# One slot for both halves of an output projection's weights, and the first half's matmuls moved behind the last attention unit

## The chip, the cores and the metric

The kernel runs on one core of a Trainium2 chip. The metric is the device time of one execution in microseconds (us), the median of several. Most runs were timed in five rounds, turn about with the kernel before on the same chip.

In the views, PE is TensorE (matmuls), PEld its weight loads, DVE VectorE, ACT ScalarE, and SPq the queue of SyncE, which issues the loads. PSUM is the memory into which TensorE accumulates. A slot is a buffer of a tile pool, and a load into it waits until the last reader of what was there is done. The granted clock is the share of TensorE's full clock that the profile records: 1.00 or 0.50 here.

## The reference, cut to what matters

One token for each of two batch rows passes a layer with two parallel branches. The attention branch projects the normalized x to 32 heads (wq), attends over the last 2048 rows of a K and a V cache with 16 heads, and projects back with wo (4096 x 576). The MLP branch has w1 (576 x 4608), a squared ReLU, and w2 (4608 x 576).

```
xn = layernorm(x)
q = xn @ wq;  p = softmax(q @ k.T / sqrt(128));  o = p @ v      # 2 x 16 heads of K and V, 2048 rows
h = relu(xn @ w1 + b1) ** 2
out = x + o @ wo + h @ w2 + b2
```

Each weight and each cache row is read once: 53.62 MB, almost all of it bf16, for two rows of output.

## The kernel before

Attention goes in 8 units of 2 MB of K and 2 MB of V. `step(u)` transposes K of unit u, and in between does the softmax of unit u-1 and PV (softmax weights times V) of an earlier unit. `pv_out(u)` takes a unit's result to its place (the rows `sm<-acc` in the timelines), and after every fourth unit `ws` is ready for one half of wo. Both halves of wo, the first three groups of w2 (nine 128-row blocks each) and the residual are accumulated in `out_ps`. The fourth group of w2 goes to another PSUM tile in four quarters that work side by side, so that little is left to do after the last load; the rest is then added to it (`part`).

```python
kvpool = ctx.enter_context(tc.tile_pool(name="kvpool", bufs=6))      # K, V and w2 groups
wbig = ctx.enter_context(tc.tile_pool(name="wbig", bufs=1))          # wq, then w1, then w2's last group
wopool = ctx.enter_context(tc.tile_pool(name="wopool", bufs=1))      # one half of wo
# ...
def out_acc(lhsT, rhs_of, start=False, stop=False):
    for i in range(2):
        pe_mm(out_ps[32 * i:32 * i + B, :], lhsT=lhsT, rhs=rhs_of(i * OH, (i + 1) * OH), ...)
# ...
def wo_acc(tq):                      # WR = 16 rows, 32 matmuls
    ws = wo_state.pop(tq)
    wo_sb = wo_tiles.pop(tq)
    for r in range(WR):
        out_acc(ws[:, r, :], lambda a, z: wo_sb[:, r, a:z])
# ...
issue_wo(1)                          # all loads of a kind go out on one queue
for w in W2P:
    issue_w2(*w)
wo_acc(0)
step(NU - 1, NU - 3, NU - 4)         # the last unit's K
# ... PV and softmax of the last two units ...
pv_all(NU - 1)
pv_out(NU - 1)
mlp_o(*W2P[0])
wo_acc(1)
for w in W2P[1:NG4 - 1]:
    mlp_o(*w)
# ... part <- out_ps; mlp_tail(rows 0 to 6); add part; mlp_tail(rows 7, 8); casts; store
```

## Time and profile before

| | kernel before |
|---|---|
| median of the first three runs | 134.18 us (134.14 to 134.27) |
| span in the profile | 132.5 us |
| TensorE busy | 91.7 us, 69% |
| transfers, share of 16 engines' time | 94.8% (the load queue) |
| end of the accumulation in `out_ps`, by the start of its copy | 127.61 us |
| release of the last w2 group's first piece | 128.43 us |

The prediction below shows the views that carry the argument. One more is wanted here: what the load queue itself waited for. Its columns are the waiting engine and line, the releaser, and the total, the number and the longest of the waits.

```profile
SPq L118 <- DMA wo<-in_A_wo_dram: 10.2, 1, 10.2
SPq L131 <- PE kT_ps L87: 8.8, 1, 8.8
SPq L118 <- PE out_ps L84: 3.4, 1, 3.4
```

Line 118 issues wo, line 131 w2 (which waits for slots of K tiles in use). The second half of wo waits for the first half to land (10.2 us) and then for its matmuls (3.4 us), because there is one slot. Such a wait of the issuing queue costs nothing as long as enough transfers are already under way.

### The profile page before, as it was taken

How to read it: one execution, taken by the hardware profiler on the slowest of the kernel's cores; microseconds unless marked ns; L12 is line 12 of the kernel's file. 1: busy time of each engine (PE TensorE's matmuls, PEld its weight loads, DVE VectorE, ACT ScalarE, POOL GpSimd, SP SyncE). 2: the span in 40 equal slices, each digit the busy share in tenths (PEclk: the TensorE clock that was granted, in tenths of full speed). 3: DMA queues.
4: the chain of work that ended last, by engine and by line, in shares of the span. 5: the costliest groups of instructions: out<-in, count | busy, mean ns of one | idle time of the engine just before them, and what ended most of it. 6: DMA issues, size and time to landing. Idle time of an engine off the chain costs nothing.

```text
span 132.5 us, 2040 instructions
## 1 busy us (share of the span) xinstructions
PE 91.7 (69%) x830; PEld 56.6 (43%) x830; DVE 59.7 (45%) x151; ACT 43.9 (33%) x63; POOL 7.7 (6%) x26
## 2 busy tenths in 40 slices
PE   0069228789762949879789389799285996449971
PEld 0059102639421439645366075465053653114540
DVE  6944301224640006565765823788700338744021
ACT  2707401016700044748357137367000733200001
POOL 7700000001000001010010000010100000100000
PEclk9999986856999595999999958999965579975698
DMA  3999989999998999999999999999999999999950
GB/s 105 443 445 501 389 381 430 430 483 513 401 403 359 430 410 455 411 460 401 465 396 445 425 415 453 415 456 432 423 410 445 415 440 433 414 432 423 418 216 1
DMA packets 3632, 53.74 MB, mean 406 GB/s; under 512 B 412, under 2 KB 420, under 8 KB 680
## 3 DMA queue, kind: packets, MB, share of 16 engines
q1 hardware_dynamic: 3604, 53.61, 94.8%
q8 instruction: 6, 0.10, 0.3%
q10 hardware_dynamic: 20, 0.01, 0.0%
q14 instruction: 2, 0.02, 0.0%
HBM read 53.62 MB, written 0.00 MB: 405 GB/s over the span
## 4 chain that ended last, share of the span: by engine, by line
DMA 71%; PE 21%; DVE 2%; ACT 2%; issue 1%; SPq 1%; DVEq 0%; ACTq 0%
DMA k<-in_A_k_cache_dram 44%; DMA w<-in_B_w_dram 13%; DMA wq_sb<-in_A_wq_dram 13%; PE kT_ps L87 10%; PE sc_ps L84 4%; PE q_ps L84 3%; PE qs_ps L84 1%; PE pv_ps L84 1%; DVE kT L288 1%; PE tail_ps L84 1%; PE sm L84 1%; ACT kT L286 1%; ACT pr L325 1%; DVE qrow L252 1%; SPq L106 0%
## 5 line engine op out<-in xcount | busy, mean ns | idle before, releaser
L87 PE MATMUL kT_ps<-ident_f,k 128*128 128x128 f32 x256 | 41.7, 322 | 6.3 <-DMA k<-in_A_k_cache_dram 6.2
L286 ACT COPY kT<-kT_ps 128x1024 bf16<-128x1024 bf16 x32 | 32.0, 1011 | 36.4 <-PE kT_ps L87 34.2
L87 PEld LDWEIGHTS kT_ps<-ident_f,k 128*128 128x128 f32 x256 | 35.2, 168 | 15.2 <-issue 12.0
L288 DVE COPY kT<-kT_ps 128x1024 bf16<-128x1024 bf16 x32 | 22.1, 692 | 31.9 <-PE kT_ps L87 31.7
L84 PE MATMUL sc_ps<-kT,qz 128*32 128x512 bf16 x128 | 10.5, 413 | 4.2 <-DVE kT L288 2.8
L84 PE MATMUL pv_ps<-v,pT 128*32 128x512 bf16 x128 | 10.9, 405 | 1.0 <-DVE acc L360 0.8
L314 POOL PARTITION_ALL_REDUCE gmax<-m x8 | 2.9, 366 | 104.3 <-DVE m L312 104.3
L84 PE MATMUL out_ps<-wo,ws 128*2 128x288 bf16 x64 | 6.8, 391 | 2.8 <-DMA wo<-in_A_wo_dram 2.8
L84 PEld LDWEIGHTS <-xnT 128*4 128x4 bf16 x90 | 3.1, 116 | 12.9 <-issue 12.7
L325 ACT ACTIVATE pr<-sc_ps,nb 128x512 bf16<-128x512 f32 x8 | 5.5, 687 | 8.1 <-DVE nb L322 8.1
L84 PE MATMUL q_ps<-wq_sb,xnT 128*4 128x512 bf16 x36 | 3.6, 573 | 4.9 <-DMA wq_sb<-in_A_wq_dram 4.9
L310 DVE TENSOR_REDUCE mx<-sc_ps 128x1 f32<-128x512 f32 x8 | 5.5, 684 | 3.1 <-PE sc_ps L84 3.1
L84 PE MATMUL h_ps<-w_sb,xnT 128*4 128x384 bf16 x54 | 4.3, 483 | 3.7 <-DMA w_sb<-in_B_w_dram 3.7
L84 PEld LDWEIGHTS <-qz 128*32 128x32 bf16 x128 | 2.3, 98 | 9.7 <-DVE kT L288 6.4
L84 PE MATMUL sm<-acc,tohead 128*64 128x129 f32 x16 | 4.0, 334 | 3.5 <-DVE acc L360 3.5
L84 PEld LDWEIGHTS <-ws 128*2 128x2 bf16 x64 | 3.7, 112 | 5.8 <-issue 3.1
L360 DVE SCALAR_TENSOR_TENSOR mix<-pv_ps,own_j,mix 128x128 f32<-128x128 f32 x16 | 5.6, 351 | 0.6
L87 PE MATMUL pro_ps<-ident,xs 2*128 2x2 bf16 x10 | 0.6, 164 | 7.6 <-DVE xs L182 7.6
L331 DVE STREAM_TRANSPOSE pT<-pr 128x512 bf16<-128x512 bf16 x8 | 5.6, 701 | 0.0
L566 ACT CAST fin_sb<-tail_ps 2x144 bf16<-2x144 f32 x2 | 0.5, 272 | 14.8 <-PE tail_ps L84 14.7
L433 DVE TENSOR_TENSOR hs<-hT_ps,hodd 128x20 f32<-128x20 f32 (+1 forms) x4 | 0.5, 173 | 10.3 <-ACT hodd L430 10.3
L84 PEld LDWEIGHTS <-pT 128*32 128x32 bf16 x128 | 2.7, 95 | 5.6 <-issue 3.0
(77 smaller groups left out, 60.4 us busy)
## 6 DMA issues: line engine op xcount, KB each, us to landing
k<-in_A_k_cache_dram SPq DMA_DIRECT2D x8, 2048.0 KB, 7.7
v<-in_A_v_cache_dram SPq DMA_DIRECT2D x8, 2048.0 KB, 17.1
w_sb<-in_B_w_dram SPq DMA_DIRECT2D x1, 5184.0 KB, 19.5
wq_sb<-in_A_wq_dram SPq DMA_DIRECT2D x1, 4608.0 KB
wo<-in_A_wo_dram SPq DMA_DIRECT2D x2, 2304.0 KB
w<-in_B_w_dram SPq DMA_DIRECT2D x3, 1296.0 KB, 19.4
w<-in_B_w_dram SPq DMA_DIRECT2D x1, 1008.0 KB
w<-in_B_w_dram SPq DMA_DIRECT2D x1, 288.0 KB
```

What stands on the lines that cost most here:

```text
L84: return tc.keep_in_program_order(nc.tensor.matmul(out, **kw))
L87: return tc.keep_in_program_order(nc.tensor.transpose(**kw))
L252: nc.vector.tensor_copy(out=qrow[:, 0, :], in_=q_ps[0][0:RB, :])
L286: pin(nc.scalar.copy(out=dst, in_=src))
L288: pin(nc.vector.tensor_copy(out=dst, in_=src))
L310: pin(nc.vector.tensor_reduce(out=mx[:], in_=sc_ps, axis=AX.X, op=ALU.max))
L314: nc.gpsimd.partition_all_reduce(gmax[:], m2[:], channels=P, reduce_op=ReduceOp.max)
L325: pin(nc.scalar.activation(out=pr[:], in_=sc_ps, func=ACT.Exp, bias=nb[:], scale=scale, accum_out=acc[:, Dh:Dh + 1]))
L331: pin(nc.vector.transpose(out=pT[:].rearrange("p t m -> p (t m)"), in_=pr[:]))
L360: op = nc.vector.scalar_tensor_tensor(out=nx, in0=pv_ps[:, j, :], scalar=own_j[:, j:j + 1], in1=acc, op0=ALU.mult, op1=ALU.add)
L433: nc.vector.tensor_tensor(out=hs[:].rearrange("p (g r) b -> p r g b", g=NG4)[:, r0:r0 + n, g:g + 2, :], in0=even[:, :, g:g + 2, :], in1=od ...
L566: cp(out=fin_sb[:, q * OQ:(q + 1) * OQ], in_=mlp["out"][32 * k:32 * k + B, :])
```

## The change

The intent: `wo_acc(0)` stands ahead of the last unit's transposes, though TensorE has idle time later, in the waits of the last PV. To move it there, the second half of wo must no longer wait for the first half's slot. Both halves together fit the slot that w1 leaves, and w2's last group, which had that slot, goes to a K/V slot. The pieces of the last group become 6 and 3 rows.

```diff
-    wopool = ctx.enter_context(tc.tile_pool(name="wopool", bufs=1))
     def issue_wo(t):
-        tl = wopool.tile([P, WR, D], BF16, tag="wo_sb", name=f"wo_{t}")
+        if t == 0:
+            wo_tiles["all"] = wbig.tile([P, B * WR, D], BF16, tag="wbig", name="wo_sb")
+        tl = wo_tiles["all"][:, t * WR:(t + 1) * WR, :]
     ...
     def issue_w2(g, r0, r1):
-        if g < NG4 - 1:
-            tl = kvpool.tile([P, FR * D], BF16, tag="kv", name=f"w2_{g}")[:]
-        else:
-            if r0 == 0:
-                w2_last.append(wbig.tile([P, FR * D], BF16, tag="wbig", name=f"w2_{g}"))
-            tl = w2_last[0][:, r0 * D:r1 * D]
+        if r0 == 0:
+            w2_rows[g] = kvpool.tile([P, FR * D], BF16, tag="kv", name=f"w2_{g}")
+        tl = w2_rows[g][:, r0 * D:r1 * D]
     ...
-    W2P = [(0, 0, 9), (1, 0, 9), (2, 0, 9), (3, 0, 7), (3, 7, 9)]
+    W2P = [(0, 0, 9), (1, 0, 9), (2, 0, 9), (3, 0, 6), (3, 6, 9)]
     ...
-    wo_acc(0)
     step(NU - 1, NU - 3, NU - 4)
     ...
     pv_all(NU - 1)
+    wo_acc(0)
     pv_out(NU - 1)
```

More of the change, by code (lines that the diff above doesn't have):

```diff
@@ L115, in issue_wo @@
     def issue_wo(t):
-        tl = wopool.tile([P, WR, D], BF16, tag="wo_sb", name=f"wo_{t}")
+        if t == 0:
+            wo_tiles["all"] = wbig.tile([P, B * WR, D], BF16, tag="wbig", name="wo_sb")
+        tl = wo_tiles["all"][:, t * WR:(t + 1) * WR, :]
         n = P * WR
-        nc.sync.dma_start(out=tl[:], in_=A_wo[t * n:(t + 1) * n, :].rearrange("(p r) n -> p r n", r=WR))
+        nc.sync.dma_start(out=tl, in_=A_wo[t * n:(t + 1) * n, :].rearrange("(p r) n -> p r n", r=WR))
         wo_tiles[t] = tl
-    w2_last = []
+    w2_rows = {}
     def issue_w2(g, r0, r1):
-        if g < NG4 - 1:
-            tl = kvpool.tile([P, FR * D], BF16, tag="kv", name=f"w2_{g}")[:]
-        else:
-            if r0 == 0:
-                w2_last.append(wbig.tile([P, FR * D], BF16, tag="wbig", name=f"w2_{g}"))
-            tl = w2_last[0][:, r0 * D:r1 * D]
+        if r0 == 0:
+            w2_rows[g] = kvpool.tile([P, FR * D], BF16, tag="kv", name=f"w2_{g}")
+        tl = w2_rows[g][:, r0 * D:r1 * D]
         rows = B_w2[g * HW:(g + 1) * HW, :].rearrange("(p r) n -> p (r n)", r=FR)
```

## The prediction

> **What bounds the kernel now.** I read the page first: the busy tenths of the DMA engines, then the chain that ended last. The first asks whether a transfer resource is full all the way through, the second whether the end hangs on it.
>
> ```profile
> DMA  3999989999998999999999999999999999999950
> ...
> DMA 71%; PE 21%; DVE 2%; ACT 2%; issue 1%; SPq 1%; DVEq 0%; ACTq 0%
> ```
>
> Thirty-seven of forty slices are at 8 or 9 tenths, only the first and the last two fall off, and 71% of the chain is transfers. 53.62 MB are read. TensorE is busy 69% and off the chain most of the time. Next the chain in order of time, for its last third:
>
> ```profile
> 74.08 27.29 DMA k<-in_A_k_cache_dram
> 101.36 0.14 issue
> 101.50 2.79 PE kT_ps L87 x12
> ...
> 110.24 0.33 SPq L131
> 110.57 0.05 issue
> 110.62 17.82 DMA w<-in_B_w_dram
> 128.43 0.04 issue
> 128.48 1.29 PE tail_ps L84 x44
> ```
>
> The last K tile is issued at 74.08 and lands at 101.36, because some 10 MB stand before it in one queue. The last group of w2 lands at 128.43, and then 1.29 us of TensorE work, two casts and the store follow. Now the timeline of the stage that the change touches (columns: start, us, engine, line, instruction, and in brackets the idle time before it with what ended it):
>
> ```profile
> 96.56 3.35 PE L84 MATMUL out_ps<-wo,ws 128*2 128x288 bf16 x32 [2.82 <-DMA wo<-in_A_wo_dram]
> ...
> 101.50 2.79 PE L87 MATMUL kT_ps<-ident_f,k 128*128 128x128 f32 x12 [1.60 <-DMA k<-in_A_k_cache_dram]
> ...
> 119.00 0.67 PE L84 MATMUL sm<-acc,tohead 128*64 128x129 f32 x2 [1.71 <-DVE acc L360]
> ...
> 119.84 2.32 PE L84 MATMUL out_ps<-w,hT_sb 128*2 128x288 bf16 x18 [0.18 <-DMA w<-in_B_w_dram]
> ...
> 121.95 3.42 PE L84 MATMUL out_ps<-wo,ws 128*2 128x288 bf16 x32
> ...
> 125.20 2.37 PE L84 MATMUL out_ps<-w,hT_sb 128*2 128x288 bf16 x36
> 127.61 0.93 DVE L555 COPY part<-out_ps 2x288 f32<-2x288 f32 x2 [6.49 <-PE out_ps L84]
> 128.48 0.61 PE L84 MATMUL tail_ps<-w,hT_sb 128*2 128x144 bf16 x28 [0.90 <-DMA w<-in_B_w_dram]
> ```
>
> The first projection (96.56 to 99.91) lies between two waits for transfers, so it does not hold up the last K tile's transposes. From 117.29 to 119.00 TensorE waits for the last mix, and from 119 to 127.6 it has no pause: it is done 0.9 us before the last w2 group comes. That slack is the number that decides this case. The windows of the same stretch show the clock (columns: window, its length, then busy us of PE, PEld, DVE, ACT, POOL, then granted clock, DMA share, GB/s):
>
> ```profile
> 114.34:117.75 3.41, 1.48 (x18) 0.52 (x18) 2.11 (x7) 0.68 (x2) 0.00 (x0) 1.00 0.95 405
> 117.75:121.16 3.41, 1.99 (x14) 1.10 (x16) 2.39 (x7) 0.00 (x0) 0.00 (x0) 0.50 1.00 426
> 121.16:124.58 3.42, 3.42 (x32) 1.81 (x28) 0.00 (x0) 0.00 (x0) 0.00 (x0) 0.50 1.01 428
> 124.58:127.99 3.41, 3.00 (x48) 1.88 (x44) 0.38 (x1) 0.00 (x0) 0.00 (x0) 1.00 0.84 343
> ```
>
> TensorE runs at half clock from 117.75 to 124.58, so its last long piece of work is slow exactly where the slack is short: 32 matmuls take 3.35 us (105 ns each) at half clock, 36 take 2.37 us (66 ns) at full.
>
> **What the Trainium skill says.** "DMA: Bandwidth & Descriptors", section Specifications, gives a ceiling of 435 GB/s for the 16 engines together. The trace agrees: these windows show 405 to 428 GB/s, and 53.62 MB over the 127 us from 1.4 to 128.4 are 422. Nothing but fewer bytes or an earlier first byte can take much off. "TensorE: Matmul & The Clock Gate", Part 1: The HAM clock gate, says that the clock is halved after an idle window and restored after a busy one, with a free-running window of 3413 ns. The trace agrees in its spacing: the granted clock changes at about 97.3, 107.5, 117.8 and 124.6, that is 3, 3 and 2 such windows apart; one with 1.48 us of TensorE work lost the clock, a full one (121.16 to 124.58) brought it back. "Perfetto Trace Analysis", section "DMA Instruction — HWDGE", says that the profiled window of a DMA instruction leaves out the movement of data. So it is here: the K issue takes half a microsecond and its data come 27 us later; I read arrivals from who waits for them.
>
> **The change part by part.**
>
> (1) *Both wo loads in w1's slot.* w1's last matmuls end near 46.5 and the first wo load goes out at 73.4, so it meets no wait. The second wo load waited 3.4 us for the first projection and went out at 99.93. Now nothing holds it, and it follows the last V load (about 86.3). The first two w2 groups then wait only for slots of the last but one K and V tiles, free near 93. But at 99.93 the queue still had the end of the last K tile and 4 MB of V, some 10 us of work at 420 GB/s. The engines never ran dry, so an earlier issue brings nothing forward: 0 us.
>
> (2) *w2's last group in a K/V slot.* It goes into the slot of V 5, whose last reader is the PV that ends at 110.75; the group before it waits, as before, for the last K tile's transposes at 110.22. Its issue moves by about 0.1 us. At that time the second wo and two w2 groups (2.3 + 1.3 + 1.3 MB, 11 us) are queued ahead: 0 us at the end.
>
> (3) *The first projection moves behind the last PV.* It leaves 96.56 to 99.91, where it was free, and starts at 117.29, where 1.71 us of waiting are. At half clock it needs 32 x 105 ns = 3.35 us. With the first 0.46 us at full clock (7 matmuls) and 25 at half, it ends at 120.4. The last pv_out (0.67) ends at 121.05 in place of 119.67: 1.4 us later. Taken alone this overdraws the 0.9 us of slack. But TensorE is now busy without a break through 117.75 to 121.16, which by the clock rule above should give the full clock at 121.16, a window earlier. Then the first w2 group takes 18 x 66 = 1.2 us (to 122.25). ws comes 1.46 us after pv_out, as the DVE rows show (119.67 to 121.13): 122.5. Second projection 32 x 66 = 2.1 (124.65). The next two groups 2.37, but the second of them lands only near 126.0 (estimate: one group, 1.33 MB, before the end, at 430 GB/s 3.1 us) and needs 1.2 after that: 127.2. So the accumulation ends at 127.2 in place of 127.6: still hidden. If the clock stays up at 117.75 (1.93 us of work in that window, between the 1.48 that lost it and the 2.03 that kept it at 110.92 to 114.34), the end is the same 127.2, set by the landing.
>
> (4) *Pieces of 6 and 3 rows.* The last bytes move at the same moment. The first piece is one row shorter, a ninth of 3.1 us = 0.34 us earlier: 128.1. Its 24 matmuls end near 128.6, the 8 of the partial sum near 129.0. The last piece: its data are through by about 128.6 in both kernels (DMA share 0.08 from 128.50, 0 from 128.75). The delay from data to release I estimate as 0.55 us (7-row data through at 128.6 - 0.7, release at 128.43), so 129.1. It has 12 matmuls in place of 8 (0.29 x 12/8 = 0.43): 129.55 in place of 129.66.
>
> Sum: 0 + 0 + 0 - 0.1 us, so 134.1 us.
>
> **Rivals.** *TensorE becomes the bound of the tail.* If the full clock comes no earlier than 124.58, the first w2 group ends at 123.4, 11 matmuls of the second projection run at 105 ns and 21 at 66 (126.0), the next groups end at 128.3, the copies (0.93) at 129.25, and the partial sum and the last piece (0.42 + 0.43) at 130.1: 0.45 us later, 134.6. For it: the windows are not tied to the program, and 2.63 us of the same projection from 97.27 to 100.68 did not restore the clock. Against it: a full window did. I give it one in four. *The earlier wo issue speeds the transfers up.* If there were gaps that the deeper queue closes, up to 1 us could come. Against it: DMA share about 1.0 in every window from 97 to 126. One in twenty. *The last K tile starts colder:* TensorE now idles from 93.7 to 101.4 whole. But the clock was already 0.50 from 97.27 to 107.51 with the projection there, so its transposes should cost the same 2.79 us.
>
> **Range and chances.** Three in four for 133.9 to 134.2, one in four for up to 134.7; the three runs of before spread 0.13 us, and I allow 0.4 below for what a different layout of tiles does to the slowest transfer engine. 2% is 2.7 us: no branch reaches it.
>
> **What would show it.** Second wo issue near 87 and not 99.93; no DMA window of 3.4 us under 0.9 between 84 and 124; release of the first piece of the last group near 128.1; the first projection at 117.3 with no idle before pv_out; full clock at about 121; the copies of the partial sum starting by 127.4. The prediction is wrong if those copies start after 128.3 (TensorE is the bound), if the chain's last transfer ends over 0.5 us from 128.4 (the transfers changed), or if a wait of the issuing queue for a slot appears after 111.

## The result, and the profile after

| run of the changed kernel | executions | median us | lowest to highest | ratio to before, 95% interval |
|---|---|---|---|---|
| first | 4 | 134.09 | 134.03 to 134.19 | 0.9987 (0.997 to 1.0004) |
| again (with the first experiments) | 6 | 134.38 | 134.07 to 134.79 | 1.001 (0.9993 to 1.0027) |
| third (with the later ones) | 6 | 134.17 | 133.96 to 134.74 | 1.0 (0.9982 to 1.0018) |

The changed kernel's 16 executions form two groups: eleven from 133.96 to 134.19, and five from 134.59 to 134.79. The executions of the kernel before, 134.05 to 134.57, leave no such gap. The first run had only the fast group. I come back to this.

First the fast group, by the profile of the first run. From its page, the busy tenths of the DMA engines and the chain by engine; then the pieces of the chain in order of time that answer to those shown of before:

```profile
DMA  4999989999998999999999999999999999999950
...
DMA 70%; PE 22%; DVE 2%; ACT 2%; issue 1%; SPq 1%; DVEq 0%; ACTq 0%
```

```profile
75.94 25.48 DMA k<-in_A_k_cache_dram
101.42 0.14 issue
101.56 2.79 PE kT_ps L86 x12
...
110.00 19.13 DMA w<-in_B_w_dram
129.13 0.04 issue
129.17 0.46 PE tail_ps L83 x12
```

The last K tile lands at 101.42 (101.36 before), and its first transposes take the same 2.79 us. The end of the chain is again a landing of w2, but now that of the last piece, at 129.13. Before, 1.29 us of matmuls hung on the first piece's landing; now 0.46 us hang on the second's. The load queue in order of time:

```profile
83.91 0.58 SPq L119 DMA_DIRECT2D wo_sb<-in_A_wo_dram  x1
94.10 16.32 SPq L129 DMA_DIRECT2D w<-in_B_w_dram  x5
```

The second half of wo goes out 16 us earlier than before (83.91 against 99.93), and yet what the end waits for lands no earlier, apart from the shorter first piece. The tail, where the moved work is:

```profile
116.74 2.89 PE L83 MATMUL out_ps<-wo_sb,ws 128*2 128x288 bf16 x32
...
119.56 0.43 PE L83 MATMUL sm<-acc,tohead 128*64 128x129 f32 x2
...
119.93 1.27 PE L83 MATMUL out_ps<-w,hT_sb 128*2 128x288 bf16 x18
...
121.52 2.12 PE L83 MATMUL out_ps<-wo_sb,ws 128*2 128x288 bf16 x32 [0.33 <-DVE ws L387]
...
123.48 1.27 PE L83 MATMUL out_ps<-w,hT_sb 128*2 128x288 bf16 x18
126.07 1.27 PE L83 MATMUL out_ps<-w,hT_sb 128*2 128x288 bf16 x18 [1.32 <-DMA w<-in_B_w_dram]
...
127.37 0.93 DVE L553 COPY part<-out_ps 2x288 f32<-2x288 f32 x2 [5.90 <-PE out_ps L83]
...
128.13 0.55 PE L83 MATMUL tail_ps<-w,hT_sb 128*2 128x144 bf16 x24 [0.80 <-DMA w<-in_B_w_dram]
...
128.60 0.42 PE L83 MATMUL tail_ps<-part,ident_f 2*2 2x144 f32 x8
...
129.17 0.36 PE L83 MATMUL tail_ps<-w,hT_sb 128*2 128x144 bf16 x12
```

Read it against the same rows of before. The moved projection starts without a wait at 116.74, and TensorE has no pause up to 121.2. The clock fell at 114.88, during the last PV, and is full again at 118.29, so the second projection takes 2.12 us in place of 3.42. Then TensorE *waits*: 1.32 us for the third w2 group, 0.80 us for the first of the last pieces. All that the move gained in TensorE time is turned into waits for transfers, and the accumulation's copy starts at 127.37, only 0.24 us earlier than before.

Now the second group of executions. The profile of the changed kernel run again fell into it (134.59 us). Its last matmuls:

```profile
125.94 1.27 PE L83 MATMUL out_ps<-w,hT_sb 128*2 128x288 bf16 x18 [1.54 <-DMA w<-in_B_w_dram]
...
127.24 0.92 DVE L553 COPY part<-out_ps 2x288 f32<-2x288 f32 x2 [6.12 <-PE out_ps L83]
...
128.00 0.89 PE L83 MATMUL tail_ps<-w,hT_sb 128*2 128x144 bf16 x24 [0.80 <-DMA w<-in_B_w_dram]
...
128.82 0.66 PE L83 MATMUL tail_ps<-part,ident_f 2*2 2x144 f32 x8
...
129.41 0.53 PE L83 MATMUL tail_ps<-w,hT_sb 128*2 128x144 bf16 x12
```

The first of the last pieces is released before 128.00, even a little earlier than in the fast execution, and the DMA share is 0.00 from 128.75 in both. But the 44 matmuls after it take from 128.00 to 129.94 in place of 128.13 to 129.53: 1.94 us against 1.40. The windows say why. I cut them at the times at which the granted clock may change in the execution concerned, which differ from one execution to the next. First the fast execution's last two, then those of the slow one (columns: window, length, busy us of PE, PEld, DVE, ACT, POOL, then clock, DMA share, GB/s):

```profile
125.12:128.53 3.41, 1.67 (x42) 1.05 (x41) 0.89 (x2) 0.00 (x0) 0.00 (x0) 1.00 0.73 297
128.53:131.94 3.41, 0.85 (x32) 0.34 (x20) 0.59 (x2) 0.55 (x2) 0.00 (x0) 1.00 0.01 2
```

```profile
124.57:127.98 3.41, 1.27 (x18) 0.70 (x17) 0.71 (x2) 0.00 (x0) 0.00 (x0) 1.00 0.85 347
127.98:131.39 3.41, 1.94 (x44) 0.89 (x44) 0.78 (x3) 0.55 (x2) 0.00 (x0) 0.50 0.05 20
```

In the slow execution a window ends at 127.98, in which TensorE worked for 1.27 us only, and the clock is halved exactly for the work that nothing hides. In the fast one the window ends 0.55 us later, has 1.67 us of work, and the clock stays. That is a reading of two profiles so far; experiments follow.

### The profile page after: what moved, and what is told of

Read it like the earlier page. It is cut to its first block, busy times and chain, and to the rows that moved or that the text cites. A ratio compares the mean times of both kernels' runs of the same rounds, so it can differ in the third digit from the quotient of the medians.

```text
span 132.3 us, 2040 instructions
## 1 busy us (share of the span) xinstructions
PE 89.0 (67%) x830; PEld 54.4 (41%) x830; DVE 59.6 (45%) x151; ACT 43.9 (33%) x63; POOL 7.7 (6%) x26
## 4 chain that ended last, share of the span: by engine, by line
DMA 70%; PE 22%; DVE 2%; ACT 2%; issue 1%; SPq 1%; DVEq 0%; ACTq 0%
DMA k<-in_A_k_cache_dram 42%; DMA w<-in_B_w_dram 14%; DMA wq_sb<-in_A_wq_dram 13%; PE kT_ps L86 11%; PE sc_ps L83 4%; PE q_ps L83 3%; PE pv_ps L83 2%; PE qs_ps L83 1%; DVE kT L286 1%; ACT kT L284 1%; ACT pr L323 1%; PE sm L83 1%; DVE qrow L250 1%; SPq L105 0%; DVE qz L266 0%
## 5 line engine op out<-in xcount | busy, mean ns | idle before, releaser
L86 PE MATMUL kT_ps<-ident_f,k 128*128 128x128 f32 x256 | 41.1, 317 | 12.4 <-DMA k<-in_A_k_cache_dram 11.8
L86 PEld LDWEIGHTS kT_ps<-ident_f,k 128*128 128x128 f32 x256 | 34.0, 164 | 21.7 <-issue 18.2
L83 PE MATMUL pv_ps<-v,pT 128*32 128x512 bf16 x128 | 11.9, 440 | 1.0 <-DVE acc L358 0.8
L83 PE MATMUL out_ps<-wo_sb,ws 128*2 128x288 bf16 x64 | 5.0, 318 | 0.3 <-DVE ws L387 0.3
L83 PE MATMUL out_ps<-w,hT_sb 128*2 128x288 bf16 x54 | 3.8, 286 | 1.3 <-DMA w<-in_B_w_dram 1.3
```

The source lines that it names most:

```text
L83: return tc.keep_in_program_order(nc.tensor.matmul(out, **kw))
L86: return tc.keep_in_program_order(nc.tensor.transpose(**kw))
```

## The experiments

Two theories were put against each other. Theory T: the transfers set the end; what the change frees on TensorE is hidden, and the slow executions come from a clock that falls because TensorE now idles ahead of the last landings. Rivals: the move itself gave the small gain; TensorE has become too full; the slow executions come from late transfers.

### The changed kernel again

No edit.

> The changed kernel once more, as the yardstick of this call. Theory (the transfers set the end, the moved work is hidden in both places): 134.1 us, ratio to the kernel before 0.998 to 1.000. Rival (the end depends on where the free-running clock window falls): some of its executions at 134.5 or more.

Measured: 134.38 us, six executions of 134.59, 134.18, 134.07, 134.79, 134.12 and 134.63. The theory's number held for three of them, and the rival named there (the free-running window) for the other three, though it acted on the last 44 matmuls, not in the accumulation.

### Slots and pieces without the move

```diff
         issue_w2(*w)
+    wo_acc(0)
     step(NU - 1, NU - 3, NU - 4)
     ...
     pv_all(NU - 1)
-    wo_acc(0)
     pv_out(NU - 1)
```

> Slots and pieces as changed, but the first projection back ahead of the last unit's transposes. Theory: the move is worth nothing at the end, so 134.1 us like the changed kernel; TensorE's accumulation ends near 127.5 again in place of 127.3 and the clock of the tail is low until about 124.6. Rival (the move is what gave the 0.14 us): 134.2 like the kernel before.

Measured: 134.13 us (133.99 to 134.26), ratio 0.9989 (0.9977 to 1.0001). So the move is not what gave the first run its 0.14 us (which are themselves not clear of noise: the interval of that ratio ends at 1.0004). The clock of the tail was low until 122.1 in this profile (the expectation said about 124.6; the window fell differently), and the accumulation's copy started at 127.31. It ran a second time, beside the changed kernel:

> Slots and pieces without the move once more, beside the changed kernel. Theory (TensorE has only 0.8 us of idle time ahead of the last accumulated group, so the clock holds): one group, 134.0 to 134.3, median 134.1. Rival (the clock falls here as often as in the changed kernel): some executions at 134.5 or more.

Measured: 134.01 us (133.92 to 134.14), ratio 0.9982 (0.9969 to 0.9995), while the changed kernel of the same call had two of six executions at 134.59 and 134.74. In ten executions of this version together none was over 134.26. Its TensorE is busier ahead of the last pieces. In the second profile the clock came back only at 124.95, and the two w2 groups ran without a wait up to the copy:

```profile
125.32 2.37 PE L83 MATMUL out_ps<-w,hT_sb 128*2 128x288 bf16 x36
127.73 0.93 DVE L553 COPY part<-out_ps 2x288 f32<-2x288 f32 x2 [7.09 <-PE out_ps L83]
```

That is the low clock and the full accumulation that the change was to do away with, and this execution still took about 134.0 us: the landing decides.

### The old pieces in the changed kernel

```diff
-    W2P = [(0, 0, 9), (1, 0, 9), (2, 0, 9), (3, 0, 6), (3, 6, 9)]
+    W2P = [(0, 0, 9), (1, 0, 9), (2, 0, 9), (3, 0, 7), (3, 7, 9)]
```

> The changed kernel with the old pieces of 7 and 2 rows. Theory (the only gain at the end is the earlier first piece): 134.2 us, 0.1 above the changed kernel, the last eight matmuls starting at about 129.4 behind the partial sum, not at 129.17 behind the landing. Rival (the pieces do nothing): 134.1.

Measured: 134.63 us (134.13 to 135.17), ratio 1.0022 (0.9999 to 1.0045). Three executions at 134.13, 134.27 and 134.37 agree with the 0.1 us, but do not show it: the interval of the changed kernel in the same call (0.9993 to 1.0027) overlaps this one. Three at 134.88 to 135.17 I count to the slow group, though they are longer than its 134.59 to 134.79. The one profile (134.92 us) is of these:

```profile
128.46 0.92 PE L83 MATMUL tail_ps<-w,hT_sb 128*2 128x144 bf16 x28 [1.16 <-DMA w<-in_B_w_dram]
...
129.31 0.66 PE L83 MATMUL tail_ps<-part,ident_f 2*2 2x144 f32 x8
...
129.90 0.41 PE L83 MATMUL tail_ps<-w,hT_sb 128*2 128x144 bf16 x8
```

The last eight matmuls start at 129.90, behind other TensorE work at half clock. The kernel before has these pieces as well, and its first row reads 0.61 where this one reads 0.92: its clock is full at that time. In the kernel before, the last eight matmuls start at 129.37, right behind the partial sum that starts at 129.02, and end at 129.66; in the changed kernel the last twelve end at 129.53. That makes the pieces the likely source of about 0.1 us. It is not shown: no run changes the pieces alone, or the slots alone, in the kernel before.

### The move alone

```diff
 (kernel before, wo keeps its own single slot)
         issue_w2(*w)
-    wo_acc(0)
     step(NU - 1, NU - 3, NU - 4)
     ...
     pv_all(NU - 1)
+    wo_acc(0)
     pv_out(NU - 1)
```

> The kernel before with the move alone: wo keeps its one slot of its own, so the second wo load waits for the first projection behind the last PV. Theory (the shared slot is what makes the move possible): the second wo load goes out near 120.5, the transfers run dry from about 111 to 122, all w2 groups come some 11 us late, 144 to 146 us. Rival (the transfers still catch up or the load is hidden): under 137 us.

Measured: 141.53 us (140.0 to 142.05), ratio 1.0522. The load queue in order of time, and one stretch of windows:

```profile
92.54 0.90 SPq L131 DMA_DIRECT2D w<-in_B_w_dram  x2
120.15 0.33 SPq L118 DMA_DIRECT2D wo<-in_A_wo_dram  x1
120.57 1.54 SPq L131 DMA_DIRECT2D w<-in_B_w_dram  x3
```

```profile
116.00:117.00 1.00, 1.00 (x14) 0.37 (x8) 0.00 (x0) 0.00 (x0) 0.00 (x0) 0.50 0.20 83
117.00:118.00 1.00, 1.00 (x14) 0.59 (x10) 0.72 (x3) 0.00 (x0) 0.00 (x0) 0.50 0.00 0
...
120.00:121.00 1.00, 1.00 (x14) 0.63 (x14) 0.45 (x3) 0.00 (x0) 0.00 (x0) 1.00 0.00 0
```

The mechanism is as expected: wo's second half waits for the moved matmuls and the engines run dry. The size was not: they stood still for some 5 us, not 11, because two w2 groups went out ahead of that load (at 92.54), though the program text has them behind it. The rest of the 7 us was not taken apart. So the shared slot, which was never run by itself, is what keeps the move from costing 7 us.

### One w2 group not loaded, in both kernels

```diff
 def issue_w2(g, r0, r1):
+    if g == 2:
+        w2_tiles[(2, 0)] = w2_tiles[(1, 0)]     # wrong result on purpose
+        return
```

In the kernel before:

> The kernel before without the load of one w2 group (the third group's matmuls read the second's tile; the result is wrong on purpose): 1.33 MB less, the transfers end some 3.1 us earlier. Theory (in the kernel before TensorE is only 0.9 us behind the transfers): TensorE becomes the bound of the tail, its accumulation still ends near 127.6, total 133.8 us, so only 0.4 us gained. Rival (TensorE is far from binding in both kernels): 131.1 us.

In the changed kernel:

> The changed kernel without the load of the same w2 group (wrong result on purpose). Theory (the move did free TensorE time, which the transfers hide): accumulation ends near 125.9, the last piece lands near 126.1, total 132.3 us, so about 1.5 us below the same cut of the kernel before. Rival (the move frees nothing): the same 133.8 us as that cut; rival (transfers bind alone): 131.0.

Measured: 133.59 us (133.03 to 134.03), ratio 0.9962, for the kernel before, and 132.8 us (132.23 to 133.02), ratio 0.9886, for the changed one; both results are wrong, as intended. With 3.1 us of transfers gone (an estimate from 1.33 MB at 430 GB/s), the kernel before gains 0.6 us, the changed one 1.4 (from the 134.17 of its third run). The ratio between the two is 0.9886 / 0.9962 = 0.9924, some 1.0 us; the medians are 0.8 us apart. TensorE is the bound in both cuts (from 119.8 on no wait for a load stands in either profile), so I read this as the TensorE time that the three parts of the change together free, and that the transfers hide in the whole kernel. I had expected 1.5. The two profiles do not show it: the accumulation's copy starts at practically the same time in them (first the cut of the kernel before, then that of the changed one), where I had expected 127.6 and 125.9.

```profile
126.72 0.92 DVE L558 COPY part<-out_ps 2x288 f32<-2x288 f32 x2 [5.95 <-PE out_ps L84]
```

```profile
126.68 0.93 DVE L556 COPY part<-out_ps 2x288 f32<-2x288 f32 x2 [4.42 <-PE out_ps L83]
```

They are the fastest of four executions (133.03 us) and one of the two slowest of four (133.01 us), so the gain rests on the times alone. In the cut of the changed kernel the profiled execution had the low clock just for the moved projection:

```profile
116.65:120.06 3.41, 3.41 (x34) 1.90 (x30) 1.40 (x4) 0.00 (x0) 0.00 (x0) 0.50 1.00 426
```

Its 32 matmuls took 3.80 us there, against 2.89 in the changed kernel's first profile, so part of the gain goes to the clock again, by where the windows fall.

### The first projection last

```diff
 (changed kernel)
-    wo_acc(0)
     pv_out(NU - 1)
     ...
     for w in W2P[1:NG4 - 1]:
         mlp_o(*w)
+    wo_acc(0)
```

> The changed kernel with the first projection moved once more, behind the last w2 group of the accumulation, where no wait is left. Theory (hidden only as long as it lies in a wait ahead of the last landing): 32 matmuls at 66 ns = 2.1 us are laid bare, accumulation ends near 129.5, total 135.9 us. If the clock is low in the tail as in the kernel before: up to 137. Rival (the transfers hide it there too): 134.1.

Measured: 135.55 us (135.47 to 136.12), ratio 1.0106 (1.0084 to 1.0128). In the profile, which is of the slowest of the four (136.12 us), the copy of the accumulation starts at 129.80:

```profile
129.80 0.93 DVE L553 COPY part<-out_ps 2x288 f32<-2x288 f32 x2 [8.96 <-PE out_ps L83]
```

By the medians the whole is 1.4 us longer than the changed kernel's fast group. TensorE time does count as soon as it lies behind the last wait; the same 32 matmuls are free only ahead of it.

### Half of the projection in the later wait

```diff
     pv_all(NU - 1)
-    wo_acc(0)
+    wo_acc(0, 0, WR // 2)
     pv_out(NU - 1)
     ...
     mlp_o(*W2P[1])
+    wo_acc(0, WR // 2, WR)
     mlp_o(*W2P[2])
```

> The changed kernel with the first projection cut in two: rows 0 to 7 behind the last PV, rows 8 to 15 (16 matmuls, about 1.06 us) in the 1.3 us wait for the last accumulated w2 group. Theory (in some executions of the changed kernel the clock falls just before the last pieces land, because TensorE idles ahead of them, and the 44 last matmuls at half clock cost 0.4 to 0.6 us): no execution over 134.4, median 134.0 to 134.1, the accumulation still ends near 127.3, clock 1.00 from 124.6 to the end. Rival (the slow executions come from late transfers): a third to a half of the executions at 134.5 to 134.8 as for the changed kernel.

Measured: 134.18 us (133.92 to 134.22), ratio 0.9987 (0.9975 to 0.9999); no execution of five in the slow group. In its profile the window that ends at 128.11 has 1.85 us of work and the clock stays full. This agrees with T, but with 5 slow ones in 16 executions of the changed kernel, five fast ones in a row would come by chance about one time in six or seven. It needed a sharper test.

### Useless work in the wait

```diff
     mlp_o(*W2P[1])
+    idle_ps = psum.tile([P, OH], F32, tag="kT", bufs=3, name="idle_ps")
+    for r in range(16):
+        pe_mm(idle_ps[0:B, :], lhsT=mlp["h"][:, r, :], rhs=wo_tiles["all"][:, r, 0:OH], ...)
     mlp_o(*W2P[2])
```

> The changed kernel with 16 useless matmuls of the same shape (about 1.06 us, into a free PSUM tile that nobody reads) in the wait for the last accumulated w2 group. Theory (idle TensorE time ahead of the landing is what lowers the clock): more work, less time: no execution over 134.4, median 134.0 to 134.1. Rival (late transfers, or TensorE too full): 134.4 or more.

Measured: 134.38 us, six executions of 134.15, 134.92, 134.56, 134.03, 134.19 and 135.04. The expectation failed, and the test was not what it was meant to be: 14 of these matmuls took 1.88 us, not 1.06 for 16, because they all wrote one column group, while the accumulation alternates between two. "TensorE: Matmul & The Clock Gate", Part 3: Packing small matmuls, says that matmuls with outputs in different column groups run side by side; the trace agrees, with 134 ns a matmul here against 72 ns (1.15 us for 16) when they alternate, below. They overran the wait, and the copy started at 127.86 in place of 127.37. The profiled execution (134.15) kept its clock, with 3.26 us of TensorE work in the window that ends at 128.57; what the three slow ones (134.56, 134.92, 135.04) had, no profile shows, and theory T did not foresee them. So I built it again with pairs:

```diff
+    for r in range(8):
+        for i in range(2):
+            pe_mm(idle_ps[32 * i:32 * i + B, :], lhsT=mlp["h"][:, r, :],
+                  rhs=wo_tiles["all"][:, r, i * OH:(i + 1) * OH], ...)
```

> The useless work of the earlier run once more, now alternating between two column groups as the accumulation does, so that 16 matmuls take about 1.1 us (one column group took some 2 us, and overran the wait by half a microsecond, which spoiled that run). Theory (TensorE's idle time ahead of the landings lowers the clock in a third of the changed kernel's executions): the last accumulated group still starts on its landing near 126.0, none of the executions over 134.4, median 134.0 to 134.15. Rival (the slow executions have another cause): about a third of them at 134.55 to 134.8.

Measured: 134.14 us, five executions from 134.12 to 134.19, ratio 0.9991 (0.9977 to 1.0005). The filler took 1.15 us and left 0.40 us of the wait. By luck its profile had windows cut almost as in the third run of the changed kernel, whose profile fell in the slow group. First that one, then the one with the filler:

```profile
124.62:128.03 3.41, 1.31 (x22) 0.74 (x25) 0.78 (x2) 0.00 (x0) 0.00 (x0) 1.00 0.78 321
128.03:131.44 3.41, 1.89 (x44) 0.84 (x44) 0.71 (x3) 0.54 (x2) 0.00 (x0) 0.50 0.05 20
```

```profile
124.70:128.11 3.41, 2.28 (x36) 1.29 (x30) 0.67 (x2) 0.00 (x0) 0.00 (x0) 1.00 0.83 338
128.11:131.52 3.41, 1.26 (x44) 0.68 (x44) 0.82 (x3) 0.54 (x2) 0.00 (x0) 1.00 0.04 15
```

Sixteen matmuls that nobody needs raise the work of that window from 1.31 to 2.28 us, the clock stays at 1.00, and the same 44 last matmuls are busy for 1.26 us in place of 1.89. The third run of the changed kernel, for completeness:

> The changed kernel beside the two above on the same chip. Theory (the free-running clock window decides): two groups again, about half of the executions near 134.1 and the rest near 134.6; median 134.1 to 134.6. Rival (the slow ones of the earlier call were that chip's): all near 134.1.

Measured: two of six executions at 134.59 and 134.74, four from 133.96 to 134.17, on another chip than the run again. The slow group is not one chip's.

With half the projection, or the paired filler, or no move at all, none of 20 executions was slow; of the changed kernel 5 of 16 were. I take the cause as shown for the profiled executions: all that fell in the slow group (two of the changed kernel, one with the old pieces) show the half clock at the end and landings that are not late (DMA share 0.00 from 128.75 in each). For executions without a profile it is an inference, and two things limit it: the changed kernel itself was not run beside the paired filler on that chip, and the three slow executions with the unpaired filler stay unexplained.

## Why the prediction was right

134.1 us was predicted and 134.09 measured, with the range right. That all four executions of that run were fast was luck in part: with 5 slow ones in 16, four fast ones in a row come about one time in four or five, and the next run's median was 134.38. By its steps:

- **Both wo loads in one slot: 0 us.** Right. The load went out at 83.91 (predicted near 87), and the last K tile and the w2 pieces landed when they had before. The move alone shows the slot's other side: without it the move costs 7 us.
- **The last group in a K/V slot: 0 us.** Right at the end. The last issue was over by 110.42, 1.1 us earlier than before, where 0.1 us of change was predicted; it made no difference.
- **The projection behind the last PV, hidden.** Right in outcome and mechanism. The copy started at 127.37 (predicted: by 127.4), with no idle time ahead of `pv_out`. Where the clock falls was left to chance, and both branches of the prediction came: in the first profile the clock fell earlier, at 114.88, and came back at 118.29, not at 121.16; in the profile of the second run the window from 114.32 to 117.74 had 1.9 us of TensorE work (1.93 in the prediction) and the clock stayed up. The copy started at 127.37 and 127.24, set by the landing as predicted. One size was wrong: 105 ns a matmul is not the half clock. The row of 3.35 us from 96.56 ran at full clock up to 97.27, and the row of 3.42 us from 121.95 from 124.58 on; its 22 matmuls before that took 2.63 us, so 120 ns each. With 120 ns the moved projection would have ended some 0.4 us later in the predicted windows, and the rival's 134.6 would be near 134.9 (estimates). The cut kernels put the freed TensorE time at 0.8 to 1.0 us, by the times.
- **Pieces of 6 and 3.** Right. Predicted were 128.1, 129.1 and 129.55 for the first release, the second and the end of the last matmuls; measured 128.09 (the trace's last arrival before the matmuls of 128.13), 129.13 and 129.53. By its own letter, one sign of being wrong came true: the chain's last transfer ended at 129.13, over 0.5 us from 128.4. But that sign was ill put: it meant the first piece, and the prediction itself has the last piece at 129.1. The transfers did not change. The same pieces without the move give the same time as the changed kernel's fast group.
- **The rival with TensorE as the bound.** One in four up to 134.7 was about the right share (5 of 16, 134.59 to 134.79, two of them above 134.7), but that is luck, for the reason was wrong. I looked for a clock that comes back too late for the accumulation. The accumulation was never late. The step that failed is "the end is the same 127.2, set by the landing": true, and I did not ask what TensorE's idle time before that landing does to the clock of the work after it. The changed kernel's TensorE is faster, so it idles more, so it can lose the clock just ahead of the 44 matmuls that nothing hides, which then take 1.94 us in place of 1.40.
- **Colder transposes of the last K tile: no change.** Right, 2.79 us both times.
- **The 435 GB/s.** The agreement holds for the mean of 422. Single windows of 3.4 us are no test of it: before, one reads 317 GB/s at a DMA share of 0.75 and another 550 at 1.27, more than the engines' whole time, so bytes are not put down to the exact moment.

What stays open: why some of the 16 DMA engines end later than others. In the changed kernel's first profile the DMA share is 0.50 from 127 to 128 and 0.19 from 128 to 129, so on average half of them, then a fifth, still move data. Each profile also has six instruction fetches of 16 KB (0.9 to 1.0 us each in the two of before and after), but no run tested whether they are the cause.

A version that looks better than both is the slots and pieces without the move: 134.13 and 134.01 us against 134.25 and 134.30 of the kernel before, ratios 0.9989 and 0.9982. Only the second interval lies clear of 1, the gain is under 0.2%, and both intervals overlap those of the changed kernel.

## What to carry to other kernels

Where transfers fill the time up to the last landing, moving engine work into an earlier wait buys nothing; count the slack ahead of that landing before you count the work. What counts is what hangs on the last landing, and the clock at which it runs: a faster TensorE ahead of it means a more idle one, and the idle time can cost some tenths of a microsecond (0.5 here). When a kernel's times fall in two groups, profile one of each before you trust a median of three.

## What the Trainium skill lacked or had wrong

- "TensorE: Matmul & The Clock Gate", Part 1, lets the clock fall after an idle window. Here a window need not be idle: 1.27, 1.31 and 1.48 us of TensorE work in 3.41 us lost it, 1.67, 1.85 and 2.28 kept it. These figures, of the last 20 us, are no threshold, since busy time alone does not decide: in the kernel before, the window from 46.07 to 49.48, with matmuls and transposes of the hidden layer in it, lost the clock with 1.68, and the one from 22.18 to 25.59, mostly small f32 matmuls, with 2.51. The page does say that the free-running window makes a kernel's start differ from run to run, but not that it can split the times of one kernel in two groups (133.96 to 134.19 and 134.59 to 134.79) where the unhidden end follows a wait.
- "DMA: Bandwidth & Descriptors", Anatomy of one DMA, puts the fixed cost at about 2 us, mostly the receipt of the last write. That was measured for DMAs issued by GpSimd, and these are issued by SyncE, so it is a difference and no contradiction. Here the DMA share is 0 from 128.75 and the last piece's matmuls are released at 129.13, so the part of it after the last byte is about 0.4 us.
